# One instruction order for another: weight-block sums moved from batch 0 to batch 1, constants built on chip, one scaling per pair of maxima

## The chip, the cores and the metric

The kernel runs on 1 core of one Trainium2 chip. The metric is the device time of that core in microseconds (us). TensorE is called PE below, VectorE DVE, ScalarE ACT, GpSimd POOL; SP is the queue from which all DMAs are issued, and it issues them strictly in its own order.

## The reference

Windowed attention with block summaries, then a gated feed-forward layer on its output.

```python
B, H, S, D = 4, 8, 768, 64          # block = 32, window = 16
k_sum = k.reshape(B, H, nb, block, D).max(axis=3)      # one key per block of 32
v_sum = v.reshape(B, H, nb, block, D).mean(axis=3)
scores_l = scale * q @ k^T, kept where |i - j| < window, else -1e9
scores_s = scale * q @ k_sum^T + log(block)
a = softmax(concat[scores_l, scores_s]);  attn = a @ concat[v, v_sum]
x = attn as (3072 tokens, 512)
g = x @ w_gate; val = x @ w_val     # 512 -> 1536
out = (g * sigmoid(g) * val) @ w_out                   # 1536 -> 512
```

The three weight matrices arrive as 64-bit floats; everything else is 32-bit.

## The kernel before

**Stages.** The work goes batch by batch (4 batches of 768 tokens, each in two halves of 384, `k = 2 * batch + half`). Per half there are 4 attention units `u`, each two heads. A unit is: `SC` scores on PE, `max0`/`max1` maxima on DVE, a scaling of the maxima by 1/8, six `exp` on ACT, `eps`, `rcp`, `nrm` (normalisation, DVE or POOL), `PP` transposes on PE, `pt` copies out of PSUM, `XO` (weights times values) on PE, and a split of the result into a high and a low part (`xh`, `xl`).

**Feed-forward.** The 1536 inner columns go in 12 chunks `j`. In batch 0 (`u_plain`) a chunk's raw 64-bit weights are loaded (`raw_w`), decoded by ACT and DVE (`abs`, `clamp`, `shift`, `sign`, `low`, each 128x1024) into a tile `m_w`, and split into a high and a low part (`hi` on ACT, `lo` on DVE or POOL, written to the tile `w`). PE then makes three products per pair of parts. In batches 1 to 3 (`u_seven`) a Strassen-like scheme needs 7 block products in place of 8, and for this four sums and differences of 128x256 blocks of each chunk's weights: `weight_sums`, the steps `sumA22`, `sumA21`, `sumA11`, `sumA12`, one after another on the same tile. Before the change they are made in batch 0 on the decoded tile `m_w` (for chunks 0 and 1 on a copy that is loaded again, `m_again`), stored to DRAM (`sf`), and in batch 1 loaded (`ls`, into the tile `s`), split (`sh`, `sl`) and stored again (`ss`) for batches 2 and 3. `down` makes the last product; its banks are called `acc`.

**What sets the order.** Each step is recorded with the engines that may do it and a cost. A planner (`order`, `run`) lays all steps out in time by these costs, after `nudge` has moved single steps by a written table of numbers (`NUDGES`); each engine then executes its steps in exactly that order. Where the planner saw PE idle in the first 110 us, it fills in warm-up matmuls on a tile `warm`.

**Start.** Constants (`raw_parts`: masks and logarithms that PE adds to the scores through `parts_sb` and an identity `id_r`; `id_sb`; `mean_sb`, the block means' matrix) are loaded by DMA. The first units on PE are SC(0,1), SC(0,3), then `pv` (block means of the values, `first_means`).

## Time and profile before

| what | value |
|---|---|
| timed runs | 678.13 us median of 3 (677.75 to 681.1) |
| profiled execution, its own time | 681.53 us |
| its span, first to last instruction | 679.8 us |
| busy share of the span | PE 98%, DVE 76%, ACT 50%, POOL 18% |
| mean granted TensorE clock | 0.995 of full speed |

The profile is of one execution; a busy PE is a stream of matmuls whose ends are modelled, so it shows gaps in the stream and not how fast the stream is. The three timed runs and the profiled one lie 3.8 us apart.

### The profile page before, as it was taken

Reading aid. Unit: us, or ns where it says so; the run is one execution under the profiler, and the core shown is the slowest. Engines: PE = TensorE matmul, PEld = TensorE weight load, DVE = VectorE, ACT = ScalarE, POOL = GpSimd, SP = SyncE. Lnnn points to the kernel's source line nnn. Section 1 sums busy time; section 2 is a strip of 40 time slices with the busy share of each in tenths; the row PEclk is TensorE's granted clock in tenths of the full one; section 3 lists DMA queues with packets and bytes.
Section 4 is the critical chain, followed back from the end, with each engine's and each line's share of the span. In section 5 each row is a group of like instructions: output and inputs, shape, how many; then the busy total and the mean of one; then the engine's idle time right before and its main releaser. Section 6 shows DMA issues by size and latency. Waiting matters only on the chain.

```text
span 679.8 us, 13325 instructions
## 1 busy us (share of the span) xinstructions
PE 667.9 (98%) x5097; PEld 616.2 (91%) x5097; DVE 513.2 (76%) x1135; ACT 340.8 (50%) x850; POOL 124.4 (18%) x115
## 2 busy tenths in 40 slices
PE   8999999999999999999999999999999999999997
PEld 8789899899899998989999898989999898989896
DVE  4899998999999786977758883766768762646464
ACT  2888757677664386644544265744535233313130
POOL 0615306504412130112413140100001000000000
PEclk8999999999999999999999999999999999999999
DMA  9999558878657588785957584663715462535232
GB/s 326 374 341 351 186 215 305 319 273 286 226 200 256 219 283 289 256 282 198 279 227 232 189 301 144 248 212 136 248 39 204 181 221 104 218 108 217 109 109 93
DMA packets 40111, 153.06 MB, mean 225 GB/s; under 512 B 4400, under 2 KB 9328, under 8 KB 33136
## 3 DMA queue, kind: packets, MB, share of 16 engines
q1 hardware_dynamic: 40048, 152.21, 63.5%
q8 instruction: 40, 0.66, 0.4%
q14 instruction: 23, 0.19, 0.1%
HBM read 116.54 MB, written 35.65 MB: 224 GB/s over the span
## 4 chain that ended last, share of the span: by engine, by line
PE 76%; DVE 11%; DMA 7%; issue 2%; ACT 2%; POOL 1%; SPq 0%; DVEq 0%; ACTq 0%; POOLq 0%
PE p L1105 37%; PE acc L1177 25%; PE g L1064 4%; PE v L1064 3%; PE sc L598 3%; PE xo L747 2%; PE pp L714 2%; DVE m_w L949 1%; DVE m_w L943 1%; DMA s<-ss 1%; DMA kw<-in_kW 1%; DMA s<-sf 1%; DVE w L489 1%; DMA raw_w<-in_wgv 1%; DVE m_w L930 1%
## 5 line engine op out<-in xcount | busy, mean ns | idle before, releaser
L1177 PE MATMUL acc<-o,hh 128*128 128x512 f32 x570 | 177.3, 392 | 0.0
L1177 PEld LDWEIGHTS acc<-o,hh 128*128 128x128 f32 x570 | 105.7, 188 | 21.9 <-issue 1.0
L1105 PE MATMUL p<-xh_T,s 128*128 128x384 f32 x432 | 122.6, 339 | 0.9 <-DVE s L489 0.4
L1177 PE MATMUL acc<-o,hl 128*128 128x512 f32 x285 | 111.4, 391 | 0.0
L1105 PE MATMUL p<-xh_B,wa 128*128 128x384 f32 x288 | 84.8, 335 | 0.0
L1105 PEld LDWEIGHTS p<-xh_T,s 128*128 128x128 f32 x432 | 79.0, 188 | 3.1 <-DMA s<-ss 1.1
L484 ACT COPY s<-p 128x384 f32<-128x384 f32 x61 | 29.2, 479 | 90.5 <-PE p L1105 83.3
L1105 PE MATMUL p<-xl_T,s 128*128 128x384 f32 x216 | 72.3, 335 | 0.0
L489 DVE TENSOR_TENSOR part<-acc,part 128x512 f32<-128x512 f32 x71 | 47.5, 685 | 29.0 <-PE acc L1177 29.0
L1177 PEld LDWEIGHTS acc<-o,hl 128*128 128x128 f32 x285 | 53.5, 188 | 11.6 <-DVE hl L489 0.3
L641 ACT ACTIVATE p<-p,nm 128x120 f32<-128x120 f32 x144 | 55.2, 385 | 11.7 <-DVE nm L629 10.2
L489 DVE TENSOR_TENSOR c<-p,u 128x384 f32<-128x384 f32 x72 | 39.6, 552 | 20.2 <-PE p L1105 20.2
L1064 PE MATMUL g<-xh_B,w 128*128 128x384 f32 x192 | 54.1, 340 | 0.4 <-DVE w L489 0.3
L1064 PE MATMUL v<-xh_B,w 128*128 128x384 f32 x192 | 53.2, 335 | 0.0
L1105 PEld LDWEIGHTS p<-xh_B,wa 128*128 128x128 f32 x288 | 53.0, 188 | 0.1
L484 ACT CAST hh<-a 128x384 fp32r<-128x384 f32 x47 | 24.1, 514 | 51.5 <-DVE a L489 47.6
L489 DVE TENSOR_TENSOR hl<-a,hh 128x384 fp32r<-128x384 f32 x77 | 45.9, 596 | 3.6 <-ACT hh L484 0.4
L1105 PE MATMUL p<-xl_B,wa 128*128 128x384 f32 x144 | 48.1, 334 | 0.0
L489 DVE TENSOR_TENSOR a<-c,a 128x384 f32<-128x384 f32 x65 | 40.7, 626 | 5.1 <-ACT a L1040 2.5
L1105 PE MATMUL p<-xh_B,s 128*128 128x384 f32 x144 | 42.4, 334 | 0.0
L1105 PE MATMUL p<-xh_T,wa 128*128 128x384 f32 x144 | 42.3, 334 | 0.0
L1105 PEld LDWEIGHTS p<-xl_T,s 128*128 128x128 f32 x216 | 40.6, 188 | 0.3
(151 smaller groups left out, 1353.8 us busy)
## 6 DMA issues: line engine op xcount, KB each, us to landing
wa<-wa SPq DMA_DIRECT2D x36, 768.0 KB, 4.3
s<-ss SPq DMA_DIRECT2D x24, 1024.0 KB, 7.2
raw_w<-in_wgv SPq DMA_DIRECT2D x12, 1024.0 KB, 6.6
ss<-s SPq DMA_DIRECT2D x12, 1024.0 KB, 7.6
wa<-w SPq DMA_DIRECT2D x12, 768.0 KB, 5.5
kw<-in_kW SPq DMA_DIRECT2D x24, 360.0 KB, 5.6
vw<-in_vW SPq DMA_DIRECT2D x28, 288.0 KB, 4.9
kt<-in_kP SPq DMA_DIRECT2D x16, 400.0 KB, 5.5
```

The costliest lines, as they stand in the source:

```text
L484: nc.scalar.copy(out, in_)
L489: vector[e].tensor_tensor(out=out, in0=a, in1=b, op=op)
L598: nc.tensor.matmul(make(sc[h])[s * QT : (s + 1) * QT, c * KC + at : c * KC + at + x.shape[-1]], make(q)[hs, qs], x, start=not biased or c ...
L641: nc.scalar.activation(out=make(p)[:, i, :], in_=make(p)[:, i, :], func=AF.Exp, scale=-1.0, bias=make(nm)[:, i : i + 1], accum_out=make(sm ...
L714: nc.tensor.transpose(make(pp)[:KC, c * P : (c + 1) * P], make(p)[:, g * NT // 2 + c, :], make(id_sb))
L747: nc.tensor.matmul(ps[hs, qs], v, make(pt)[:, h, qs], start=True, stop=True)
L930: lambda e: nc.vector.tensor_scalar(out=make(m), in0=make(m), scalar1=F64_LO, scalar2=F64_HI, op0=ALU.max, op1=ALU.min), (), (m,),
L943: lambda e: nc.vector.scalar_tensor_tensor(out=bits(), in0=high(), scalar=-0x40000000, in1=bits(), op0=ALU.bitwise_and, op1=ALU.bitwise_or ...
L949: lambda e: nc.vector.scalar_tensor_tensor(out=bits(), in0=low(), scalar=29, in1=bits(), op0=ALU.logical_shift_right, op1=ALU.bitwise_or), ...
L1064: nc.tensor.matmul(t[:, :TOK], a, x, start=u == order_of[0] and i == 0, stop=u == order_of[-1] and i == 2,)
L1105: nc.tensor.matmul(t[:, :TOK], a, x, start=first and kk == 0 and n == 0, stop=kk == 1 and n == 2, skip_group_check=not first,)
L1177: nc.tensor.matmul(ps[:, :wide], a, w, start=j == js[0] and m == 0, stop=j == js[-1] and m == 2)
```

## The change

Six things change. (1) For chunks 3 to 11 the four block sums are no longer made in batch 0. The decoded tile goes to DRAM as it is, and batch 1 loads it into a new tile `sm` (one buffer), makes the sums there, and splits from it. Chunk 2 is as before; chunks 0 and 1 are loaded again for their sums at chunks 10 and 11 and no longer at 5 and 6. (2) In batch 0 the six maxima of a unit are scaled by one instruction after both maxima, and not by one for each three. (3) The three constants are made by memsets and by POOL's `affine_select`, and their DMAs are gone. (4) The planner lets a step on DVE, ACT or POOL that waits for a DMA start 2.5 us later than it thinks the DMA lands (`SAFE`, for landings between 60 and 215 us). (5) Where a step may go to several engines, DVE is charged 0.3 us more than before, and `join` may now go to ACT. (6) The table of nudges is another one.

```diff
+BY_EXP = 0
+ONE_SCALE = True
+SUMS_LATER = 3
-AGAIN = 5
+AGAIN = 10
...
+SAFE, SAFE_FROM, SAFE_TO = 2.5, 60.0, 215.0
-BIAS = {DVE: 0.0, ACT: 0.0, POOL: 0.3}
+BIAS = {DVE: .3, ACT: 0.0, POOL: 0.3}
...
-kt(0,1) -217.9; q(0,1) -205.2; raw_parts -367.5; id_sb -346.1; mean_sb -133.9; vn(1) -330; vr(1) -256.6
+kt(0,1) -92.5; q(0,1) -47; kt(0,3) -57; q(0,3) +18.5; kt(0,0) +51.4; q(0,0) +23.5; kt(0,2) +55.6; vn(0) +57.9
...
+        more = SAFE if s.engine == DMA and SAFE_FROM < s.end < SAFE_TO else 0.0
         for o in s.next:
-            at[o] = max(at[o], (s.end + lag) if o.after[s] else s.start)
+            at[o] = max(at[o], s.end + lag + more * (not {PE, DMA} & set(o.engines)) if o.after[s] else s.start)
...
+    def add_choose(name, b, part, cols, to, pattern, base, keep, other, rows=1):
+        plan.add(
+            name, {POOL: 0.1 + 0.0012 * cols},
+            lambda e: nc.gpsimd.affine_select(
+                out=to(), in_=to(), pattern=pattern, compare_op=keep, fill=other, base=base, channel_multiplier=rows,
+            ), (), ((b, part),),
+        )
+
+    def make_constants():
+        masks = lambda: make(raw_parts)[:, : 3 * KC].rearrange("p (v c) -> p v c", c=KC)
+        add_fill("id one", id_sb, None, P, lambda: make(id_sb), 1.0)
+        add_choose("id here", id_sb, None, P, lambda: make(id_sb), [[-1, P]], 0, ALU.is_equal, 0.0)
+        logs = log_parts()
+        for x, to in enumerate((lambda: masks()[:, :, KW:], lambda: make(raw_parts)[:, 3 * KC : 3 * KC + NB], lambda: make(raw_parts)[:, 3 * KC + NB :])):
+            add_fill(f"log{x}", raw_parts, f"l{x}", NB, to, logs[x])
+        add_fill("mask none", raw_parts, "m", 3 * KW, lambda: masks()[:, :, :KW], 0.0)
+        for s in range(2):
+            rows = slice(s * QT, (s + 1) * QT)
+            to = lambda rows=rows: masks()[rows, :, :KW]
+            add_choose(f"mask{s} above", raw_parts, "m", 3 * KW, to, [[0, 3], [-1, KW]], 2 * WIN - 1, ALU.is_ge, MASK)
+            add_choose(f"mask{s} below", raw_parts, "m", 3 * KW, to, [[0, 3], [1, KW]], -1, ALU.is_ge, MASK, rows=-1)
+        add_fill("mask first", raw_parts, "m", WIN, lambda: masks()[:QT, 0, :WIN], MASK)
+        add_fill("mask last", raw_parts, "m", WIN, lambda: masks()[QT:, 2, WIN + QT : KW], MASK)
+        add_fill("mean all", mean_sb, None, NV * NB, lambda: make(mean_sb), 1.0 / BLK)
+        add_choose("mean above", mean_sb, None, NV * NB, lambda: make(mean_sb), [[P, NV], [-BLK, NB]], -WIN, ALU.is_ge, 0.0)
+        add_choose("mean below", mean_sb, None, NV * NB, lambda: make(mean_sb), [[-P, NV], [BLK, NB]], WIN + BLK - 1, ALU.is_ge, 0.0, rows=-1)
...
-                plan.add(f"scl{g}({k},{u})", {DVE: 0.14, ACT: 0.18}, lambda e, g=g: shrink(e, g), (), ((nm, g),))
+                if not ONE_SCALE:
+                    plan.add(f"scl{g}({k},{u})", {DVE: 0.14, ACT: 0.18}, lambda e, g=g: shrink(e, g), (), ((nm, g),))
+                elif g == 1:
+                    plan.add(f"scl({k},{u})", {DVE: 0.14, ACT: 0.18}, lambda e: shrink(e, None), (), (nm,))
...
-            weight_sums(j, m)
+            if j < SUMS_LATER:
+                weight_sums(j, m)
+            keep_sums(j, m)
...
-            add_dma(f"ls({b},{j})", P * NC * 4, lambda: lo().bitcast(F32), lambda: make(SF[j]), (SF[j],), ((s, 1),))
-            add_copy(f"sh({j})", (ACT, DVE), NC, hi, lambda: lo().bitcast(F32), ((s, 1),), ((s, 0),))
+            whole, part = (lambda: lo().bitcast(F32)), (s, 1)
+            if j >= SUMS_LATER:
+                part = buf("tmp", "sm", [P, NC], f"sm{j}", room="tmp")
+                whole = lambda part=part: make(part)
+            add_dma(f"ls({b},{j})", P * NC * 4, whole, lambda: make(SF[j]), (SF[j],), (part,))
+            if j >= SUMS_LATER:
+                weight_sums(j, part)
+            add_copy(f"sh({j})", (ACT, DVE), NC, hi, whole, (part,), ((s, 0),))
             plan.add(
                 f"sl({j})", on((DVE, POOL), "tt", NC),
-                lambda e: minus(e, lo(), lo().bitcast(F32), hi().bitcast(F32)), ((s, 0),), ((s, 1),),
+                lambda e: minus(e, lo(), whole(), hi().bitcast(F32)), ((s, 0), part) if j >= SUMS_LATER else ((s, 0),), ((s, 1),),
```

The order moves at many places. The first shown is the start of the SP queue. `kt` are a unit's keys, `q` its queries, `vn` value rows, `raw_w` a chunk's raw weights. Before:

```order
L503 DMA raw_parts<-in_parts 128x408
L503 DMA id_sb<-in_ident 128x128
L503 DMA vn_99<-in_vN 128x1536
L503 DMA vn_99<-in_vR 32x256
L503 DMA kt_1_106<-in_kP 128x800
L503 DMA q_1_108<-in_qP 128x384
L503 DMA kt_3_110<-in_kP 128x800
L503 DMA mean_sb<-in_mean 128x168
```

And after the change:

```order
L496 DMA kt_1_107<-in_kP 128x800
L496 DMA kt_3_119<-in_kP 128x800
L496 DMA q_1_127<-in_qP 128x384
L496 DMA vn_131<-in_vN 128x1536
L496 DMA vn_131<-in_vR 32x256
L496 DMA q_3_172<-in_qP 128x384
L496 DMA q_0_174<-in_qP 128x384
L496 DMA q_2_176<-in_qP 128x384
```

The constants' DMAs are gone and unit 1's queries stand third in the queue and no longer sixth, behind two loads of keys.

The second place is DVE's start after the change, with the semaphores that each row waits for. The first rows fill the constants; `ks` are a unit's block keys, without which its scores can't be finished.

```order
L519 MEMSET raw_parts 128x3x24
L519 MEMSET raw_parts 128x3x96
L519 MEMSET raw_parts 128x24
L519 MEMSET mean_sb 128x168
L519 MEMSET raw_parts 64x16 [waits DVE_49,Pool_49]
L519 MEMSET raw_parts 64x16 [waits Pool_49]
L568 TENSOR_REDUCE ks_1_133<-kt_1_107 128x24 [waits DMAHW0_49]
L568 TENSOR_REDUCE ks_3_135<-kt_3_119 128x24 [waits DMAHW1_49]
```

The two 64x16 fills are new, wait for POOL's seven selections, and stand in DVE's queue ahead of the first `ks`.

The third place is DVE in batch 1, around chunk 4: `s_4` is that chunk's split tile, `sm_3328` the tile of chunk 5, `c`, `a`, `u`, `hl` are work on the feed-forward of chunks 2 and 3. Before:

```order
L489 TENSOR_TENSOR s_3_3207<-s_3_3207 128x1024 [waits DVE_49]
L489 TENSOR_TENSOR hl_2_1_3316<-a_2_1_3294,hh_2_1_3307 128x384 [waits Activation_49]
L817 TENSOR_REDUCE vr_2_3320<-vt_2_2534 128x24 [waits DMAHW4_49]
L486 CAST s_4_3271<-s_4_3271 128x1024 [waits DMAHW6_49,DMAHW1_49]
L489 TENSOR_TENSOR s_4_3271<-s_4_3271 128x1024 [waits DVE_49]
```

And after the change:

```order
L482 TENSOR_TENSOR hl_2_1_3302<-a_2_1_3259,hh_2_1_3296 128x384 [waits Activation_49]
L479 COPY part_0_3309<-acc_0_0_3220 128x512 [waits PE_49]
L482 TENSOR_TENSOR s_4_3304<-sm_3193,s_4_3304 128x1024 [waits DMAHW4_49,Activation_49]
L846 TENSOR_REDUCE vr_3_3326<-vt_3_3281 128x24 [waits DMAHW0_49]
L482 TENSOR_TENSOR sm_3328<-sm_3328 128x256 [waits DMAHW2_49,DVE_49]
L482 TENSOR_TENSOR sm_3328<-sm_3328 128x256 [waits DVE_49] x3
L482 TENSOR_TENSOR u_1_3_3396<-p_1_3_3363,s_1_3_3394 128x384 [waits Activation_49]
```

Four sums of chunk 5 now stand on DVE one row behind the split of chunk 4, and the load of `sm` for chunk 5 can be issued only when that split is done, since there is one buffer. Over the program the block sums on DVE go from 26 in batch 0 to 8 there and 25 in batch 1; on POOL from 22 to 4 and 11.

## Rows read from the trace of the kernel before

**Rows 1.** The page's busy times over the span: us, share, instructions.

```profile
PE 667.9 (98%) x5097; PEld 616.2 (91%) x5097; DVE 513.2 (76%) x1135; ACT 340.8 (50%) x850; POOL 124.4 (18%) x115
```

**Rows 2.** Stretches (us from the start): length, then busy us of each engine (instructions), granted clock, DMA share, GB/s. The last two are batch 1 and batches 2 and 3.

```profile
36.10:55.30 19.20, 18.17 (x262) 16.75 (x258) 19.20 (x29) 16.39 (x41) 4.20 (x4) 1.00 0.97 361
55.30:82.00 26.70, 25.71 (x243) 23.07 (x244) 26.21 (x43) 20.71 (x50) 14.48 (x11) 1.00 0.72 247
82.00:119.00 37.00, 37.00 (x244) 35.23 (x243) 32.20 (x68) 23.64 (x49) 10.21 (x8) 1.00 0.74 259
119.00:153.00 34.00, 33.77 (x263) 30.30 (x262) 33.80 (x74) 24.10 (x55) 11.30 (x10) 1.00 0.83 295
153.00:221.00 68.00, 67.50 (x561) 61.76 (x560) 66.71 (x153) 42.33 (x102) 22.61 (x19) 1.00 0.71 242
226.10:382.60 156.50, 156.05 (x1158) 143.93 (x1157) 121.48 (x293) 82.62 (x213) 35.67 (x32) 1.00 0.74 253
382.60:673.40 290.80, 290.33 (x1875) 270.62 (x1874) 183.07 (x430) 110.69 (x271) 12.56 (x15) 1.00 0.48 170
```

**Rows 3.** What PE waited for: us in total, times, longest.

```profile
PE sc L598 <- DMA q<-in_qP: 1.3, 1, 1.3
...
PE g L1064 <- DVE xl_B L489: 0.9, 1, 0.9
```

**Rows 4.** PE in order of time (start, us, what): the first scores of SC(0,1) and of SC(0,3), the two `pv`, the first `g`.

```profile
8.97 0.35 PE L598 MATMUL sc<-kt,q 64*64 64x96 f32 x2 [1.32 <-DMA q<-in_qP]
...
11.38 0.62 PE L598 MATMUL sc<-kt,q 64*64 64x96 f32 x8
...
15.02 3.31 PE L772 MATMUL pv<-vn,mean_sb 128*24 128x128 f32 x28
...
21.68 1.83 PE L772 MATMUL pv<-vn,mean_sb 128*24 128x128 f32 x28
...
36.14 0.44 PE L1064 MATMUL g<-xh_B,w 128*128 128x384 f32 x1
```

**Rows 5.** Stretches of the start, columns as in rows 2; the last number is GB/s.

```profile
0.00:6.00 6.00, 4.96 (x29) 4.97 (x30) 0.67 (x3) 1.28 (x1) 0.19 (x4) 1.00 0.63 190
6.00:7.00 1.00, 1.00 (x11) 1.00 (x11) 0.00 (x0) 0.00 (x0) 0.00 (x0) 1.00 1.05 380
0.00:16.00 16.00, 13.61 (x164) 12.88 (x166) 6.67 (x14) 3.96 (x14) 0.19 (x4) 0.86 0.89 319
11.40:18.20 6.80, 6.80 (x85) 5.52 (x84) 3.84 (x10) 2.16 (x12) 0.00 (x0) 0.50 1.03 410
```

**Rows 6.** DMA issues: count, KB of each, median us from issue to landing.

```profile
raw_w<-in_wgv SPq DMA_DIRECT2D x12, 1024.0 KB, 6.6
...
kt<-in_kP SPq DMA_DIRECT2D x16, 400.0 KB, 5.5
q<-in_qP SPq DMA_DIRECT2D x32, 192.0 KB, 5.7
...
vn<-in_vN SPq DMA_DIRECT2D x2, 768.0 KB, 7.3
```

**Rows 7.** The chain of work that ended last (start, us, what): its first transfer, and the load and split of one chunk's sums in batch 1.

```profile
3.04 5.80 DMA q<-in_qP
...
313.33 7.02 DMA s<-sf
...
321.10 1.24 DVE s L489
322.38 7.57 PE p L1105 x42
```

**Rows 8.** DVE in order of time: the first block keys `ks`, the first `lo` of a weight chunk, and the low part of the last unit of half 1.

```profile
8.34 0.95 DVE L542 TENSOR_REDUCE ks<-kt 128x24 f32<-128x768 f32 x1 [0.54 <-DMA kt<-in_kP]
...
34.73 1.21 DVE L489 TENSOR_TENSOR w<-m_w,w 128x1024 fp32r<-128x1024 f32 x1
...
80.89 0.54 DVE L489 TENSOR_TENSOR xl_B<-xo,xh_B 128x384 fp32r<-128x384 f32 x1
```

**Rows 9.** Instructions on the decoded tile `m_w`: count, ns min/median/max, first and last start, shape. The 128x256 rows are the block sums.

```profile
L489 DVE TENSOR_TENSOR m_w<-m_w x22: 405/411/1224, 60.1 to 205.5; 128x256 f32<-128x256 f32 x22
L489 POOL TENSOR_TENSOR m_w<-m_w x18: 732/1080/3275, 54.2 to 195.9; 128x256 f32<-128x256 f32 x18
L926 ACT ACTIVATE m_w<-raw_w x12: 1122/1156/1212, 23.6 to 192.2; 128x1024 f32<-128x1024 f32 x12
...
L943 DVE SCALAR_TENSOR_TENSOR m_w<-raw_w,m_w x12: 1176/1216/2348, 28.1 to 196.8; 128x1024 int32<-128x1024 int32 x12
...
L484 ACT CAST w<-m_w x12: 1045/1052/1092, 32.4 to 199.6; 128x1024 fp32r<-128x1024 f32 x12
```

**Rows 10.** POOL in order of time: a one-input copy of 384, the first two-input instruction of the run (720 wide), and a later one of the same shape.

```profile
20.75 0.50 POOL L486 COPY vw<-vn 64x384 f32<-64x384 f32 x1
...
26.86 1.70 POOL L693 TENSOR_TENSOR p<-p,ri 128x720 f32<-128x720 f32 x1
...
66.47 1.38 POOL L693 TENSOR_TENSOR p<-p,ri 128x720 f32<-128x720 f32 x1
```

**Rows 11.** Between 222 and 400 us, all DMAs into or out of `s`: issue to landing.

```profile
DMA to landing us min/median/max: 3.9/7.0/11.2
```

**Rows 12.** What DVE waited for between 222 and 400 us: us in total, times, longest.

```profile
DVE s L486 <- DMA s<-sf: 2.9, 3, 1.7
```

159 lines of the change are left out of this document (83 added, 76 removed).

## The prediction

> **What bounds it now.** I read the busy times first: PE is busy 98% of the span, DVE 76% [rows 1]. With PE near full, a change pays only where PE's stream has gaps, so I cut the span into stretches [rows 2]. From 82 us to 673.4 us PE idles 0.50 us up to 153, 0.50 up to 221, 0.45 in batch 1 and 0.47 in batches 2 and 3: about 2 us in 591. Between 36.1 and 82 us it idles 1.03 + 0.99 us. Before 36 lies the long start: the first scores wait for their queries until 8.97 us, and the first feed-forward product `g` begins at 36.14 [rows 4]. The waits say what ends the start's gaps: first the DMA of `q`, at the end of the start the low part `xl_B` from DVE [rows 3]. DVE is busy 19.20 of 19.20 us between 36.1 and 55.3, and 26.21 of 26.70 up to 82 [rows 2], and the `xl_B` that PE waits for ends at 81.43 [rows 8]. So up to 82 us the kernel goes by DVE, which was fed late; behind that, by PE's own work, which the change leaves as it is. PE's matmuls are the same in number and shape in both orders.
>
> The profiled execution took 681.53 us: 679.80 of span and 1.73 around it. That is 3.40 above the median of the timed runs. I make the sum against 681.53 and carry the difference over to 678.13.
>
> **Step 1, the queue's start.** Unit 1's queries stood behind 204 + 64 + 768 + 32 + 400 KB, with their own 192 KB 1660 KB = 1.70 MB (sizes of `kt`, `q` and `vn` [rows 6], the others from their shapes). The queue moved 1.14 MB in 6 us and then 0.38 a us [rows 5], so their bytes were through at 7.5; they landed at 3.04 + 5.80 = 8.84 [rows 7], 1.35 later. After the change 400 + 400 + 192 KB = 1.02 MB stand in front: through at about 5.6, landed at 7.0. SC(0,1) can begin 1.9 us sooner, if its keys and constants are there.
>
> The constants now come from POOL: seven selections of 4 x 288 + 128 + 2 x 168 = 1616 elements a row, an operation that no row shows. The nearest rows bound it: a copy of 384 took 0.50 us (1.3 ns an element), a block sum of 256 1.08 us at the median (4.2 ns) [rows 9, 10]. That gives 2.1 to 6.8 us; a selection has one input, as the copy, so I take 3. POOL then ends at about 4, between 3 and 7.5. Two fills on DVE wait for it, and behind these stands `ks` with 0.95 us [rows 8]: PE has what it needs between 4.1 and 8.6. At 3 us the making is hidden under the `q` transfer; without that cover it costs at most 8.6 - 7.0 = 1.6, and still nothing against 8.97.
>
> **Step 2, the first weights.** With 4 keys, 4 queries and both value tiles ahead, 4992 KB = 5.11 MB go through until the first `raw_w` is there. The queue had moved 319 x 16 = 5.1 MB at 16 us [rows 5], so it lands at 17.4. Chunk 0 is decoded alone, no longer abreast with chunk 1: `abs` 1.16 to 18.6, two scalings and two combinations of 1.2 on DVE among other rows to about 23.5 [rows 9]. ACT has the third `raw_w`'s `abs` ahead of `hi`; that load ends with 7.21 MB, at 0.41 a us [rows 5] at 21.1 + 1.35 = 22.4, so `hi` ends at 22.4 + 1.16 + 1.05 = 24.7 and `lo` at 26. Before, the first `lo` ended at 35.94 [rows 8].
>
> This is not 10 us won: DVE did other chunks' rows meanwhile. The fair mark is the last `xl_B`. In the order, DVE has 70 rows between the first `lo` and it before, and 78 after. Before, they took 81.43 - 35.94 = 45.5 us, 0.65 a row; 78 rows take 50.7, and from 26 that gives 76.7: 4.7 us sooner. The eight further rows hold more normalisations and fewer small rows than the mean; counted by kind they are some 1.5 us dearer, which leaves 3.2. I take 4.0, with 1 (PE or a transfer is late next and holds DVE) and 6.5 (all rows of DVE come at once) as bounds.
>
> **Step 3, the sums leave batch 0.** 26 sums on DVE become 8: 18 x 0.41 = 7.4 us. 22 on POOL become 4: 18 x 1.08 = 19.4 us [rows 9]. Nearly all lies behind 82 us, where PE has 37.00 of 37 us, 33.77 of 34 and 67.50 of 68 [rows 2]. The work that hides it is PE's own stream; the most that can come back is 0.73 us and the small hitches within the stream. I take 1.0, bounds 0 and 2. The reserve behind DMAs and the bias to ACT only say who does what when; DVE is busy 33.80 of 34 and 66.71 of 68 us there [rows 2], so it hardly waits for a DMA, and they too are worth at most this. The scaling removes eight small instructions, and lets three `exp` of a unit wait for the second maximum; DVE is ahead of ACT in both orders: 0.
>
> **Step 4, the sums come to batch 1.** 25 x 0.41 = 10.3 us on DVE, 11 x 1.08 = 11.9 on POOL. DVE has 156.5 - 121.5 = 35 us free there [rows 2], so the load fits. What matters is the loop of the single `sm` buffer: load 7.0 [rows 11], four sums 1.6 (DVE) to 3.0 (two of them on POOL), `sh` 1.05 as a cast of this size on ACT [rows 9], `sl` 1.24 [rows 7]: 10.9 to 12.3 us. PE takes 156.5 / 12 = 13.0 for a chunk. It fits, with 1 to 2 us to spare. Behind the first sum that waits in DVE's queue stands `u` of the next chunk, and PE waits for its bank. Before, DVE waited 2.9 us in three places on this load [rows 12], and the 7.02 us load on the chain let PE start at 322.38 [rows 7]. I charge 0.5, bounds 0 and 4.
>
> **Sum.** 681.53 - 4.0 - 1.0 + 0.5 = 677.0; against the median 678.13 - 4.5 = **673.6 us**.
>
> TensorE's clock was at half (1.2 GHz) from 11.4 to 18.2 us [rows 5], after PE had idled before 8.97; `pv` took 3.31 us there and 1.83 later [rows 4]. After the change the ten warm-ups ahead of SC(0,1) are gone and PE idles longer before it, so such a stretch may come again or fall otherwise. PE's work in it grows by some 2 to 3 us; it is covered as long as DVE sets the end of the start. If not, up to 3 us of step 2 are lost, which its lower bound holds.
>
> **Rivals.**
> *The constants are late* (0.10). What speaks for it: DVE's `ks` stands behind POOL. If POOL needs 6 us more than I take, SC(0,1) starts at 4 + 6 + 1.1 = 11.1, 2.1 later than before; step 2's gain is gone, the first attention is 2 us late, of which the early `raw_w` hides part: about 678 to 680, say 679. Against it: the first two-input instruction on POOL, in front of which a configuration instruction stands in the order of before, took 1.70 us beside 1.38 of a later one [rows 10], so 0.3 for the first call. The Trainium skill (GPSIMD Engine Reference, Instruction dispatch) says that a first call to freshly loaded code costs about 6 us that no instruction shows; by that rule this rival comes true. The trace does not agree with it for that first call.
>
> *The start's gain is given back* (0.10). DVE is ahead, but the next `raw_w` can only come when PE has freed a slot, so DVE waits and is where it was. For it: DVE's load to the last `xl_B` is the same in sum. Against: PE too is ahead by then. 681.53 - 0.5 carries over as 677.6.
>
> *Batch 1 stalls: slower* (0.16). If the load of `sm` takes 10 us, between the median and the longest of 11.2 [rows 11], the loop is 10 + 3.0 + 1.05 + 1.24 = 15.3, 2.3 over PE's 13.0. Nine chunks make 20.7; one chunk's products, 7.57 us [rows 7], are buffered, so 13 us arrive: 673.1 + 13 = 686. It begins to cost at a loop of 13.9 and makes the kernel slower by 0.5% at 14.8, a load of 9.5. For it: one buffer, DMAs in order in one queue. Against: half of the transfers on `s` landed in 7.0 us or less, and the tile's load no longer waits for a slot of `s`.
>
> *More is won* (0.12): the full 6.5 of step 2 and 2 of step 3, and 0 for step 4: 678.13 - 8.5 = 669.6.
>
> **How the numbers follow.** My forecast has 0.52 and spans 671 to 676.6 by the nearer half of its bounds. A measurement of this kernel tells about 0.5% (3.4 us) from no change, so faster is below 674.7. Of the 0.52, 0.38 lie there and 0.14 in no change. Faster: 0.38 + 0.12 = 0.50. Same: 0.14 + 0.10 + 0.10 = 0.34. Slower: 0.16. The range leaves out a part of the slower case and the far end of the better one: 667.5 to 681.
>
> **What would show it.** Step 1: SC(0,1) at about 7, POOL's selections over by 5, `q` landing at 7. Step 2: the first `lo` ends at 26, `g` begins at 31 to 34, and the last `xl_B` ends near 77. Step 3: PE's busy time between 82 and 221 no fuller than now. Step 4: DVE waits for `sm` of 1 to 3 us and PE waits below 1. I'd be wrong if PE's gaps in batch 1 sum to several us, if selections begin only at 7 us, or if DVE idles before 80 us.

## The result and the profile after

| kernel | median (spread, runs) | before beside it | ratio, 95% interval |
|---|---|---|---|
| changed | 684.12 us (682.63 to 684.75, 6) | 678.26 us (median of 6) | 1.0075 [1.0059, 1.009] |

The change makes the kernel slower by 5.9 us; 673.6 was predicted, with a range up to 681. The profiled execution took 684.49 us, 682.7 of them span. Of all executions below, one of a_xo took 1590.25 us, at full clock; its ratio leaves that one out, and no run says why.

The page's busy times after, to be held against [rows 1]:

```profile
PE 667.3 (98%) x5077; PEld 614.0 (90%) x5077; DVE 503.9 (74%) x1087; ACT 378.5 (55%) x905; POOL 127.4 (19%) x129
```

DVE lost 9.3 us of work and ACT gained 37.7, as the change says. PE's share says nothing; the stretches do. After, columns as in [rows 2]:

```profile
55.30:82.00 26.70, 24.84 (x300) 21.56 (x299) 26.21 (x42) 20.61 (x49) 6.24 (x5) 1.00 0.70 242
82.00:119.00 37.00, 37.00 (x246) 35.50 (x245) 36.33 (x71) 25.85 (x51) 2.34 (x3) 1.00 0.79 282
119.00:153.00 34.00, 34.00 (x268) 31.03 (x267) 33.87 (x66) 23.24 (x51) 12.66 (x9) 1.00 0.75 260
153.00:221.00 68.00, 67.33 (x562) 61.93 (x561) 56.80 (x135) 41.66 (x103) 16.88 (x16) 1.00 0.74 255
226.10:382.60 156.50, 154.01 (x1142) 140.96 (x1142) 125.30 (x294) 98.55 (x236) 51.90 (x51) 1.00 0.73 247
```

Batch 0 is a little fuller (0.23 us more between 119 and 153), its end not, and in batch 1 PE idles 2.49 us instead of 0.45. What PE waited for, columns as in [rows 3]:

```profile
PE pp L743 <- DVE p L722: 2.5, 3, 1.3
PE sc L624 <- DMA q<-in_qP: 2.1, 1, 2.1
...
PE p L1161 <- DVE v L482: 1.1, 1, 1.1
...
PE acc L1233 <- DVE hl L482: 0.7, 1, 0.7
...
PE p L1161 <- DVE part L482: 0.4, 1, 0.4
```

The first two are the start (PE waits for the normalisation `nrm`, the tile `p`, at 31.88, 34.98 and 53.14 us); the other three are new and lie in batch 1. PE in order of time, answering [rows 4]; a bracket is the idle time ahead of a row and what ended it:

```profile
8.03 0.42 PE L624 MATMUL sc<-kt,q 64*64 64x96 f32 x8 [2.12 <-DMA q<-in_qP]
...
10.84 2.91 PE L1274 MATMUL sc<-warm 128*128 128x128 f32 x12
13.68 0.62 PE L624 MATMUL sc<-kt,q 64*64 64x96 f32 x8
...
213.70 1.62 PE L776 MATMUL xo<-pt,vw 120*64 120x64 f32 x48
...
226.54 0.42 PE L1161 MATMUL p<-xh_T,s 128*128 128x384 f32 x1 [0.42 <-DVE part L482]
...
242.04 0.45 PE L1161 MATMUL p<-xh_B,s 128*128 128x384 f32 x1 [1.10 <-DVE v L482]
...
376.47 0.50 PE L1233 MATMUL acc<-o,hl 128*128 128x512 f32 x1 [0.69 <-DVE hl L482]
```

SC(0,1) starts at 8.03 and not at 7; SC(0,3) at 13.68, later than the 11.38 of before, because a warm-up group stands ahead of it. DVE in order of time, answering [rows 8]: the first `lo`, the last `xl_B` of the start, and the rows that PE waited for.

```profile
29.32 1.23 DVE L482 TENSOR_TENSOR w<-m_w,w 128x1024 fp32r<-128x1024 f32 x1
...
81.39 0.55 DVE L482 TENSOR_TENSOR xl_B<-xo,xh_B 128x384 fp32r<-128x384 f32 x1
...
214.66 0.56 DVE L479 COPY xf<-xo 128x384 f32<-128x384 f32 x1 [1.85 <-PE xo L776]
...
225.72 1.27 DVE L482 TENSOR_TENSOR part<-acc,part 128x512 f32<-128x512 f32 x2
...
240.82 0.69 DVE L479 CAST s<-s 128x1024 fp32r<-128x1024 f32 x1 [2.89 <-DMA q<-in_qP]
...
375.05 1.36 DVE L482 TENSOR_TENSOR hl<-a,hh 128x384 fp32r<-128x384 f32 x1
```

The first `lo` ends 5.4 us sooner than before (30.55 against 35.94), and the last `xl_B` 0.5 us later.

**Where the time went.** The matmuls are the same in every order, so I give each shape its usual length in the stream (128x384: 173 ns), add them up without the warm-ups (649.7 us in all), and ask when each trace has done a given amount. This is an estimate: with other lengths for the small shapes the differences between traces move by up to half a microsecond or so. The columns are the time at 60 us of work (the start is over), what 60 to 200 takes (batch 0), 200 to 340 (batch 1) and 340 to 400 (its end and the beginning of batch 2).

| trace | to 60 | 60-200 | 200-340 | 340-400 | span |
|---|---|---|---|---|---|
| before | 84.0 | 141.3 | 140.2 | 60.0 | 679.8 |
| before again | 84.0 | 140.3 | 139.5 | 60.0 | 678.3 |
| after | 84.6 | 139.6 | 142.2 | 62.1 | 682.7 |
| after again | 84.8 | 139.6 | 141.0 | 62.2 | 683.7 |

From the table: the start gained nothing, batch 0 some 0.7 to 1.7 us, and the two stretches from 200 to 400 lost 3.0 to 4.8 (3.7 between the two "again" rows). The two "again" rows come from the runs b_again and a_again below; from 400 on, `after` lost nothing against `before`, and a_again some 1.6 us, 1.3 of it in two waits for loads of `s`.

### The profile page after: what moved, and what is told of

It reads as the page before. It is cut to its first block, busy times and chain, and to the rows that moved or that the text cites. A ratio compares the mean times of both kernels' runs of the same rounds, so it can differ in the third digit from the quotient of the medians.

```text
span 682.7 us, 13319 instructions
## 1 busy us (share of the span) xinstructions
PE 667.3 (98%) x5077; PEld 614.0 (90%) x5077; DVE 503.9 (74%) x1087; ACT 378.5 (55%) x905; POOL 127.4 (19%) x129
## 4 chain that ended last, share of the span: by engine, by line
PE 75%; DVE 8%; DMA 3%; ACT 2%; issue 1%; POOL 0%; SPq 0%; DVEq 0%; ACTq 0%
PE p L1161 34%; PE acc L1233 24%; PE g L1119 5%; PE v L1119 4%; PE xo L776 3%; PE pp L743 2%; PE sc L624 2%; DMA s<-sf 1%; DMA s<-ss 1%; DVE xl_T L482 1%; DVE part L482 1%; DVE hl L482 1%; DMA q<-in_qP 1%; DVE xf L482 1%; DVE p L722 0%
## 5 line engine op out<-in xcount | busy, mean ns | idle before, releaser
L477 ACT CAST hh<-a 128x384 fp32r<-128x384 f32 x71 | 36.2, 513 | 63.0 <-DVE a L482 60.2
L482 DVE TENSOR_TENSOR hl<-a,hh 128x384 fp32r<-128x384 f32 x79 | 47.6, 602 | 13.0 <-ACT hh L477 10.5
L482 DVE TENSOR_TENSOR u<-p,s 128x384 f32<-128x384 f32 x36 | 19.9, 554 | 30.0 <-ACT s L477 28.4
L482 POOL TENSOR_TENSOR hl<-a,hh 128x384 fp32r<-128x384 f32 x17 | 20.5, 1211 | 110.6 <-ACT hh L477 63.8
```

Of the source, the lines that this page charges most:

```text
L477: nc.scalar.copy(out, in_)
L482: vector[e].tensor_tensor(out=out, in0=a, in1=b, op=op)
```

## The experiments

Orders are changed behind the planner, by taking named steps out of the finished order and putting them ahead of others (`move(name, ahead_of)`), so that all other steps stay as they were.

### The two kernels again, and the clock of an execution

**b_again** and **a_again** are the kernels unchanged.

> The kernel before once more, unchanged, for a second trace and for the spread of its times. Every theory expects 678.3 us, within 1 us. The first trace of before took 681.5, 3.3 above the median of its runs. If that was a single disturbed execution, this trace has a span near 676.5, and PE in the kernel after the change falls behind it by 5 to 6 us and not by 3; the stretch in which the two traces of before part shows where the 3 us were lost.

> The kernel after the change once more, unchanged: a second trace of it and the spread of its times beside the three below. Every theory expects 684.1 within 1 us. The two earlier traces with its order (without warm-ups, without the sums) lose the same four places: 0.6 us at P7 of chunk 0 (225 us), 0.4 at P7 of chunk 8 (323), 1.1 to 1.3 at the last products of batch 1 (375 to 380); the 1.3 us at 240.6 was in the first trace of after alone. If they are the order's, they stand in this trace too; the one at 240.6 need not.

b_again: 678.7 us, ratio 0.9993 [0.9977, 1.0008]. a_again: 682.59 us (680.21 to 685.43, 8), ratio 1.0052 [1.0032, 1.0073]. So the loss is between 3.4 and 5.9 us.

Each timed execution shows its mean granted clock. In five sets of runs, the 111 executions of before part in two: 85 with 0.998 or more, with medians of 678.3 to 679.0 in a set, and 26 below, with medians of 680.6 to 681.0, so 1.6 to 2.7 us longer, 2.5 in the middle set. Both profiles of before belong to the second kind; their stretch at half clock is [rows 5]. So the prediction's starting point was a start that before has in one execution of four. Two runs show what decides it.

**a_nowarm**, the changed kernel without the warm-ups from SC(0,1) on (the eleven ahead of everything stay):

```diff
-            spare[0] = min(30, max(0, int((s.idle - 0.5) / 0.25)))
+            spare[0] = 0
```

> The kernel after the change, same order, without the warm-up matmuls that are filled in from SC(0,1) on (the eleven ahead of everything stay). Theory 1 (the start's gain is eaten by warm-ups at half clock: the six ahead of SC(0,3) take 2.9 us, 10.8 to 13.7): SC(0,3) begins near 11, the first `lo` 1 to 2 us sooner, and 1 to 3 us of the end are won: 681 to 683. Rival (the start is set by what DVE and ACT get from the queue, and PE only waits where it now warms up): 684.1 within 0.7. A third way, against both: with less work PE stays at half clock longer, and the time grows by 1 to 3 us.

683.81 us (681.05 to 685.5, 8), ratio 1.0061 [1.0038, 1.0084]; all eight executions at 0.995 or less. Its trace is of the fastest, at 0.995; six of the eight ran at 0.984 to 0.989. **b_fill**, before with 15 warm-ups ahead of SC(0,1) and not 10:

```diff
+            if s.name == "SC(0,1)":
+                spare[0] = 15
```

> The kernel before, same order, with fifteen warm-ups ahead of SC(0,1) and not ten, so that PE is busy until its queries land. What it tells: in the kernel before, 12 of 49 timed executions had a mean clock below 0.998 and were 1.6 to 2.6 us slower. If the idle 1.3 us ahead of SC(0,1) brings the half clock on, it is gone here: all clocks at 0.998 or more, median 678.2 to 678.6 and a narrow spread. Its trace is then that of the start of before at full clock: theory 1 (the new start is no faster at equal clock) expects PE's work of the first 84 us to be done 2.0 to 2.6 us sooner than in the slow trace of before, at 81.5 to 82, where the start after the change stood at 82.5 with full clock. Rival (the new start is faster at equal clock): 83 to 84.

678.57 us, ratio 0.9984 [0.9964, 1.0004]; all twelve executions at 0.999 or more. Stretches of the trace of b_fill, then of a_nowarm, then of the changed kernel:

```profile
11.40:18.20 6.80, 5.97 (x142) 5.29 (x141) 5.44 (x15) 4.58 (x25) 2.15 (x3) 1.00 1.03 409
```

```profile
20.00:27.00 7.00, 5.50 (x68) 5.11 (x70) 6.75 (x11) 6.08 (x20) 4.88 (x5) 0.55 1.00 407
```

```profile
9.00:15.00 6.00, 6.00 (x67) 5.72 (x64) 2.19 (x4) 2.37 (x13) 1.45 (x3) 0.50 1.03 404
```

The number before the DMA share is the granted clock: 1.00 where the warm-ups fill PE's wait, 0.55 in a later stretch where there are none, and 0.50 (1.2 GHz) in the changed kernel, behind the 2.12 us that PE waits for `q`. Before and b_fill together show the cause: with PE's wait filled, the slowed executions are gone. The price, some 2.5 us, is the distance between the two kinds of before. It doesn't explain the change: three executions of after at full clock have a median of 683.33, three at less 684.21; for a_again they are 682.3 and 682.88.

### The start

**a_fill**: the changed kernel with 8 warm-ups ahead of SC(0,1) and none, for six, ahead of SC(0,3).

```diff
+            if s.name == "SC(0,1)":
+                spare[0] = 8
+            elif s.name == "SC(0,3)":
+                spare[0] = 0
```

> The kernel after the change with eight warm-ups ahead of SC(0,1), where PE stood idle 2.1 us for its queries, and none ahead of SC(0,3), where six stood. Theory 1 (PE's idle 2.1 us brings the half clock, and that eats the start's gain): the granted clock stays full in most executions, SC(0,3) begins at 10.5 and not at 13.7, and the median falls by 1 to 2.5 us, to 681.6 to 683.1, with a narrower spread. Rival (DVE and ACT set the end of the start, and PE has time to lose): 684.1 within 0.7, with or without the half clock.

682.04 us, ratio 1.0039 [1.0025, 1.0053]: 0.55 us less than a_again beside it, within the intervals. The start's warm-ups are not where the loss is.

**b_onchip**: the old order with the constants made on chip and the first keys and queries drawn forward, and nothing else of the change.

```diff
...
+    for name, do in (("raw_parts", make_parts), ("id_sb", make_id), ("mean_sb", make_mean)):
+        by[name].do = do
+    move("mean_sb", "vn(1)")
+    move("kt(0,1)", "vn(1)")
+    move("q(0,1)", "vn(1)")
```

> The kernel before in its own order, but the three constants are made on chip (same fills and selections as after the change, at the head of DVE's and POOL's rows), their three DMAs are gone, and unit 1's keys and queries go first in the queue. It takes the first step alone. SC(0,1) begins at 7.7 (its ten warm-ups end at 7.6) and not at 8.97; the half clock may fall elsewhere. If the start's lead reaches the end, 677.0 to 677.3; if it is given back, 678.3 within 0.7; if an earlier SC(0,1) only brings the half clock on sooner and longer, 679 to 680.

679.1 us, ratio 1.0016 [0.9993, 1.0038]: the constants on chip neither cost nor win anything that can be measured. Four of its ten executions ran at 0.995 or less (median 681.38), the other six took 678.27.

Stretches from 0 to 36.1 us, of b_again, of after, of b_fill, of a_nosums (below) and of b_on2 (below); DVE's busy time is the fourth number behind the bounds:

```profile
0.00:36.10 36.10, 32.12 (x473) 28.62 (x473) 24.44 (x46) 20.25 (x72) 11.58 (x17) 0.91 0.93 349
```

```profile
0.00:36.10 36.10, 30.54 (x425) 27.67 (x426) 23.97 (x48) 22.12 (x73) 12.44 (x24) 0.91 0.91 334
```

```profile
0.00:36.10 36.10, 32.42 (x492) 29.92 (x493) 26.04 (x48) 21.12 (x73) 10.49 (x17) 1.00 0.95 362
```

```profile
0.00:36.10 36.10, 30.71 (x469) 26.90 (x470) 26.90 (x52) 24.88 (x77) 12.98 (x24) 0.95 0.96 353
```

```profile
0.00:36.10 36.10, 33.00 (x517) 30.35 (x518) 27.59 (x56) 22.99 (x77) 14.27 (x24) 1.00 0.95 364
```

DVE has worked 24.44, 23.97, 26.04, 26.90 and 27.59 us by then, and these traces have done 60 us of PE's work at 84.0, 84.6, 82.3, 81.8 and 81.1: in these five a microsecond of DVE's work done early goes with about one won at the end of the start. It is not exact: b_onchip, with 27.65 us of DVE, stands at 81.8. This is the row that the prediction should have forecast. With a start that is not slowed from 9 us on, the new order (a_nosums 81.8, a_nowarm 82.6, a_fill 82.5) is about level with the old one (b_fill 82.3, b_onchip 81.8). Two things weaken this: the three traces of the new order have a shorter stretch at half clock later, between 16 and 28 us, and those of a_nosums, a_nowarm, b_onchip and b_on2 are each the fastest execution of their run. So an early first `lo` wins little here; that other rows, which come later, pay for it is argued and not shown.

### The sums

**a_nosums** leaves out the 36 block sums of chunks 3 to 11; loads, splits and stores stay.

```diff
+    for j in range(SUMS_LATER, NJ):
+        for x in ("A22", "A21", "A11", "A12"):
+            done.remove(by[f"sum{x} w{j}"])
```

> The kernel after the change, same order, without the 36 block sums of chunks 3 to 11: they are left out of the computation (the scheme of batches 1 to 3 then works on wrong blocks), all loads, splits and stores stay. Theory 2 (step 4 was sized too small: the sums' work on DVE and POOL in batch 1 is what makes PE wait there): the stalls at 240.6 and 375 to 379 us shrink and 3 to 4 us come back: 680 to 681. Rival (what stalls is the order of rows and the landing of loads, which the sums don't touch; the largest stall, at 240.6, is on chunk 2, whose sums were made in batch 0): 683 to 684.1.

682.58 us, ratio 1.0052 [1.0033, 1.0072], between the two ranges expected and nearer the rival's. Without the work that step 4 charges, the kernel is as slow as a_again. PE in order of time in a_nosums shows the same two waits, 2.8 and 4.3 us sooner since its start and some of its stream were shorter:

```profile
223.77 0.41 PE L1161 MATMUL p<-xh_T,s 128*128 128x384 f32 x1 [0.45 <-DVE part L482]
```

```profile
372.18 0.50 PE L1233 MATMUL acc<-o,hl 128*128 128x512 f32 x1 [0.70 <-DVE hl L482]
```

**a_sums0** does the opposite: the changed kernel's order, but each chunk's sums made in batch 0, behind its `lo`.

```diff
...
+            s.do = lambda e, j=j, to=to, x=x, y=y, op=op: tt(e, *(make(MW[j])[:, cols[c]] for c in (to, x, y)), op)
+            move(s.name, f"wa{j}")
+        move(f"sf{j}", f"wa{j}")
```

> The kernel after the change with the 36 block sums of chunks 3 to 11 put back into batch 0, on the engines that had them in batch 1, each behind the chunk's `lo` and ahead of the store; the rest of the order stays. It undoes the first of the six changes alone. My steps 3 and 4 said that batch 0 would pay 1.0 for them and batch 1 be relieved by 0.5. From the run without the sums, where batch 1 gained 0.3 to 0.7, I expect batch 1 to gain 0.5, and batch 0 to lose 0 (if PE's stream hides them, as before the change) or 1 to 3 (if DVE, with fewer free places in this order, makes PE wait): 682.1 to 685.

702.73 us, ratio 1.0331 [1.0296, 1.0367], far outside the range expected. From 82 to 153 us PE is busy 62.77 us of 71 and the longest wait is 6.5:

```profile
82.00:153.00 71.00, 62.77 (x439) 56.63 (x439) 65.11 (x114) 40.75 (x72) 13.31 (x11) 0.93 0.58 201
```

```profile
PE acc L1233 <- DVE part L482: 6.5, 1, 6.5
```

That shows that this order was laid out without room for the sums in batch 0. It doesn't show what they cost an order made for them: before has them there and is busy 70.77 us in the same stretch [rows 2].

### The two ends of batch 1

Two views name what stands ahead of the wait at 226. The engines between 205 and 230 us, in b_again and in a_again (DVE is the fourth number behind the bounds):

```profile
205.00:215.00 10.00, 10.00 (x56) 9.60 (x55) 9.90 (x24) 4.14 (x10) 0.00 (x0) 1.00 0.91 298
215.00:230.00 15.00, 15.00 (x74) 13.25 (x73) 11.13 (x17) 3.68 (x8) 6.77 (x4) 1.00 0.50 192
```

```profile
205.00:215.00 10.00, 10.00 (x89) 9.18 (x89) 4.73 (x11) 3.72 (x9) 0.00 (x0) 1.00 0.53 195
215.00:230.00 15.00, 14.58 (x86) 12.45 (x81) 14.19 (x21) 6.94 (x14) 8.06 (x6) 1.00 0.57 208
```

The old order has DVE busy 9.90 and then 11.13 us; the new one leaves it idle for half of the first ten and fills the next fifteen to 14.19. Part of the reason is one pair of steps. `XO(3,2)` and `XO(3,3)`, the last attention products of batch 0, stood ahead of the last chunk's `g`; the new table puts them behind two of the last six `D0` (the final products of batch 0). b_again's PE:

```profile
202.75 1.62 PE L747 MATMUL xo<-pt,vw 120*64 120x64 f32 x48
```

After, it is 213.70 (above), and the copy `xf<-xo` waits until 214.66. Several of batch 1's first inputs (`t`, `xh_T`, `xl_T`) wait for these copies, so their rows fall together with the `part` rows that empty PE's banks.

**a_mend** moves 16 rows on DVE, ACT and POOL at the three waits, and leaves XO where it is. Four of them:

```diff
...
+        ("T2l(1,0)", "part(0,3,4)"), ("T2l(1,1)", "T4(1,1)"), ("T4(1,0)", "T4(1,1)"), ("T4h(1,0)", "T4(1,1)"),
...
```

> The kernel after the change with 16 rows moved at the three places where PE waits in every trace of its order: the sums into `part` of batch 0 ahead of two low parts of the next batch's blocks, two sums of chunk 7 ahead of a normalisation and of an `hl`, and `hl` of chunk 11 ahead of the next batch's block sums, which go behind it. Nothing else moves. Theory 3 (batch 1 is slower because of where DVE's rows stand, not because the sums are more work): 0.6 + 0.4 + 1.1 come back, 682.0 beside 684.1 of after on this chip. Theory 2 (DVE and POOL have too much to do in batch 1): the rows that are put back are late next, PE waits for them, and less than 0.7 comes back.

682.35 us, ratio 1.0055 [1.0035, 1.0076]: nothing won. PE in order of time, and a stretch:

```profile
375.78 0.39 PE L1233 MATMUL acc<-o,hl 128*128 128x512 f32 x1
378.08 1.20 PE L1233 MATMUL acc<-o,hh 128*128 128x512 f32 x2 [1.92 <-DVE part L482]
379.07 0.63 PE L1233 MATMUL acc<-o,hl 128*128 128x512 f32 x1
...
378.00:380.00 2.00, 1.92 (x5) 1.55 (x6) 2.00 (x5) 0.00 (x0) 0.00 (x0) 0.54 0.57 207
```

The wait moved to the next row of a full DVE and grew, and behind it the same matmul took 0.63 us in place of 0.39 for some 3 us: the granted clock was 0.54 between 378 and 380 us and 0.61 between 380 and 382. So a_mend may have won something at its three places and lost it to this stop; its trace is of one execution.

**a_xo** moves the transposes for both XO back ahead of the last `g`, both XO (in its trace at 208.73) and their copies ahead of the last `v`, the first rows of batch 1 ahead of the last `mul` of batch 0, and rows at the end of batch 1 ahead of others there, 34 steps in all:

```diff
...
+        ("PP0(3,2)", "g(11,1)"), ("PP1(3,2)", "g(11,1)"), ("PP0(3,3)", "g(11,1)"), ("PP1(3,3)", "g(11,1)"),
...
+        ("XO(3,2)", "v(11,1)"), ("XO(3,3)", "v(11,1)"),
...
+        ("T4h(2,1)", "mul(1,11,1)"), ("B22l(2,0)", "mul(1,11,1)"), ("B22l(2,1)", "mul(1,11,1)"), ("T4l(2,1)", "mul(1,11,1)"),
...
```

> The kernel after the change with rows moved at the two batch boundaries. From batch 0 to 1: the transposes and results of the last attention pair, XO(3,2) and XO(3,3), go back ahead of the last `g` and `v` on PE, about where they stood before the change, and seven rows on their results go ahead of the last `mul`. From 1 to 2: `hl` of chunk 11 ahead of the next batch's low parts, as in the run before, but now the three sums into `part` also go ahead of them. Theory 3 (the order leaves DVE idle for 5 us ahead of the boundary and full behind it): the 0.6 us at P7 of chunk 0 and the 1.1 to 1.3 at the last products of batch 1 are gone and nothing takes their place: 680.7 to 681 beside 682.6 of after. Theory 2 (DVE is full there whatever the order): they turn up at another row again, 682.6 within 0.7.

680.63 us, ratio 1.0014 [0.9994, 1.0034], where a_again had 1.0052 [1.0032, 1.0073]; the intervals just touch. Its stretches, and a wait that is left:

```profile
205.00:215.00 10.00, 10.00 (x99) 9.18 (x97) 5.45 (x12) 6.06 (x14) 3.04 (x3) 1.00 0.43 168
215.00:230.00 15.00, 15.00 (x75) 13.32 (x74) 11.61 (x21) 5.00 (x10) 2.96 (x3) 1.00 0.61 226
...
374.00:381.00 7.00, 6.94 (x31) 5.23 (x30) 5.83 (x12) 1.54 (x3) 1.29 (x2) 1.00 0.39 149
...
321.57 0.44 PE L1161 MATMUL p<-xh_T,s 128*128 128x384 f32 x1 [0.22 <-DVE c L482]
```

Behind 215 us DVE has 11.61 us where it had 14.19, PE is full, and the wait near 376 is gone too. In the ten microseconds before, DVE is still idle for almost half: what helped is the relief behind them, not the filling of that idle time. PE's work from 200 to 400, by the table's reckoning:

| before-type: before / b_again / b_on2 | after / a_again / a_nowarm / a_nosums / a_fill / a_mend | a_xo / a_xofill |
|---|---|---|
| 200.2 / 199.5 / 199.5 | 204.3 / 203.2 / 202.8 / 202.9 / 203.6 / 205.6 | 201.2 / 201.2 |

Every trace of the new order takes at least 202.8 there, with the sums or without them; with both ends mended 201.2. So by this reckoning 2.0 us of a_again's 3.7 are the two ends; how they share it was not run. Part of the other 1.7 lies at the wait for `c` of the view above, which stands in after (at 323.92), a_again and a_xo alike and in neither trace of before; no run removes it alone, and the rest stays without a name.

**a_xofill** is a_xo with the warm-ups of a_fill:

> The kernel after the change with both repairs that helped: the rows at the two batch boundaries moved, and eight warm-ups ahead of SC(0,1) in place of six ahead of SC(0,3). If the two causes (the half clock at the start, 0.5 us in the median by the run that filled it, and the order at the boundaries, 2.0 to 2.5) add up and are most of what was lost, it comes to 679.6 to 680.3 beside 678.8 of before, and what is left is below 0.2%. If the clock was the smaller part of the two only because the boundaries hid it, up to 1 us lower; if the repairs don't add, 680.6.

680.08 us, ratio 1.002 [1.0004, 1.0035]: the changed kernel mended at three places is still not faster than before.

### The table against the five other parts

**a_empty** and **b_empty** are the two kernels with an empty table, so that the planner's own order runs:

```diff
-NUDGES = """
...
+NUDGES = """"""
```

> The kernel after the change with an empty table of nudges: the planner's own order with the five other changes in it. Beside the next run it tells whether the changes themselves or the written table lost the time. Theory 3 (it is the table's order that leaves the boundaries badly placed): with neither table the new version is not slower than the old one, by 0 to 4 us faster. Rival (sums in batch 1, the reserve or the bias are bad in themselves): it is 3 us or more slower than the old one without its table. Both are expected above the tuned ones, at 685 to 705.

> The kernel before with an empty table of nudges, to stand beside the run above. Theory 3 expects it at or above the new version without a table, the rival 3 us or more below; both expect 685 to 705.

| | its own table | empty table |
|---|---|---|
| before | 678.45 | 701.44, ratio 1.0336 [1.0316, 1.0355] |
| after | 684.12 and 682.59 | 682.0, ratio 1.0054 [1.0039, 1.007] |

Both were expected at 685 or more, and after with an empty table is below that. Its trace has XO early again:

```profile
201.61 1.62 PE L722 MATMUL xo<-pt,vw 120*64 120x64 f32 x48
```

PE is full from 205 to 230 us, so it is the new table that moved XO. But between 200 and 440 us PE now waits for `v` (0.5 us) and twice for `s` (0.5 and 0.4), and the kernel is no faster: without the table other waits take the place of its two.

**a_esums** is a_empty with the sums back in batch 0 (and chunks 0 and 1 loaded again at 5 and 6), **a_ebias** a_empty without the reserve and the bias:

```diff
-SUMS_LATER = 3
+SUMS_LATER = 12
-AGAIN = 10
+AGAIN = 5
```

```diff
-SAFE, SAFE_FROM, SAFE_TO = 2.5, 60.0, 215.0
+SAFE, SAFE_FROM, SAFE_TO = 0.0, 60.0, 215.0
-BIAS = {DVE: .3, ACT: 0.0, POOL: 0.3}
+BIAS = {DVE: 0.0, ACT: 0.0, POOL: 0.3}
```

> The kernel after the change with an empty table, and one more thing undone: the block sums are all made in batch 0 again (and chunks 0 and 1 loaded again at 5 and 6), as before the change. Without tables the new version took 682.0 and the old one 701.4. Theory 4 (the sums are what fills DVE in batch 0 where no table has fitted them in; my step 3 then had the right mechanism and its price was already paid by the old table): this kernel loses most of the 19.4 us again, 695 to 702. Rival (the bias, the reserve or the start make the difference): 682 to 686.

> The kernel after the change with an empty table and without the reserve behind DMAs (2.5 us made 0) and without the bias of 0.3 us against DVE; the sums stay in batch 1. Theory 4 (the sums make the difference): 682 to 685. Rival (the planner's reserve and bias do): 690 to 702.

691.22 us, ratio 1.0193 [1.0168, 1.0218], and 688.15, ratio 1.0139 [1.0114, 1.0164]: neither fell into a range expected, since both parts count. In the planner's own order the sums in batch 1 are worth 9.2 us, reserve and bias 6.2, all five parts 19.4. But the old table is worth 23.0 us to the old kernel, and the new table nothing to the new one. I read this so: the tuned old order has by its table what the five parts bring to an untuned one, and nothing is left for them to win. No run puts the five parts under the old table, so this is argued from four medians.

### A version that beats both

**b_best** drew all of the start of b_onchip further forward (it also has the three lines shown for b_on2 below), with no warm-ups ahead of SC(0,1) and five behind:

```diff
+    move("kt(0,3)", "vn(1)")
+    move("q(0,3)", "vn(1)")
...
+            if s.name == "SC(0,1)":
+                spare[0] = 0
+            elif s.name == "FV(0)":
+                spare[0] = 5
```

> The kernel before in its own order with constants made on chip, and with the start drawn forward: keys and queries of units 1 and 3 go first in the queue, ahead of the values; the two copies of unit 3's windows that waited for the values stand behind the first softmax; no warm-ups ahead of SC(0,1), five ahead of the second block means. SC(0,1) begins at 5.9 to 6.2, 3 us sooner than before, and SC(0,3) at 8. If an earlier start reaches the end, 676 to 677 beside 678.5 of before; if what is won is given back by the first weights, which come only 1.7 us sooner, 677 to 678.5; if PE's thinner work brings the half clock more often, 679 to 680.

679.26 us, ratio 1.0 [0.9987, 1.0014]. SC(0,1) began at 6.1, but all twelve executions ran at 0.997 or less: PE idled 2.38 us ahead of 16.61, and the clock was 0.66 between 16 and 21. **b_on2** is b_onchip with the ten warm-ups kept, two copies of unit 3 behind the first softmax and two small copies on ACT:

```diff
+    move("odd1(3)", "exp0(0,3)")
+    move("odd2(3)", "max0(0,3)")
+    by["parts"].engine = by["idr"].engine = ACT
```

> The kernel before in its own order, with constants made on chip, unit 1's keys and queries first in the queue, and the two copies that stood in front of its block keys moved behind the first softmax; the ten warm-ups stay and now reach to the scores, so that PE has no idle time before them. It joins the two things that helped the old order: full clock (678.57 where the queue was as before) and 0.5 us of start (82.3 to 81.8 at 84 us of PE's work). Expected 677.7 to 678.2 beside 678.8 of before, all clocks at 0.998 or more. Rival: 678.5, if the start's 0.5 us doesn't reach the end.

677.78 us, ratio 0.9992 [0.998, 1.0004], with 11 of 12 executions at 0.999 or more. One wait of [rows 3] was left, PE in order of time:

```profile
78.61 0.45 PE L1064 MATMUL g<-xl_B,w 128*128 128x384 f32 x1 [1.00 <-DVE xl_B L489]
```

On DVE a 1.21 us row of `m_o` and a 0.94 us `vr` stood ahead of this `xl_B`. **b_final** moves them behind it:

```diff
+    for name in ("low o4", "vpool(1,1)", "hi o4"):
+        move(name, "lo o4")
```

> The kernel before with constants on chip and the start drawn together, as in the run that took 677.8, and with three rows put behind the last low part `xl_B` of half 1, for which PE waited 1.0 us at 78.6 us in that run's trace: `low` of an output weight, a sum over value rows, and `hi` of that weight. `xl_B` can then start at 76.2, when its high part is done, and not at 78.0. If nothing behind the moved rows is waited for, 1.0 us comes off: 676.6 to 677.0 beside 678.5 of before, 0.2 to 0.3% faster. Rival: `low` and `hi` are late next for the first output products, and it stays at 677.8.

677.27 us (676.18 to 679.45, 12), ratio 0.9975 [0.9962, 0.9988]. PE does not wait between 60 and 90 us any more. It is faster than before by a quarter of a per cent, or 1.1 us against before's executions at full clock beside it (678.37), and thus faster than the changed kernel too. It has a full clock at the start, constants on chip, a queue and two copies drawn together and three rows of DVE moved; what each is worth is below what these runs can tell apart.

## Why the prediction was wrong, step by step

**Step 1** was right on the constants and off on the transfer. POOL's first and last selections:

```profile
1.52 0.44 POOL L525 TENSOR_SCALAR_AFFINE_SELECT raw_parts<-raw_parts 64x288 f32<-64x288 f32 x1 [0.47 <-DVE raw_parts L519]
...
3.93 0.44 POOL L525 TENSOR_SCALAR_AFFINE_SELECT raw_parts<-raw_parts 64x288 f32<-64x288 f32 x1
```

They are over at 4.37 (forecast: about 4), and the seven take 2.78 us (forecast: 3). The rival "the constants are late" falls. The extra of about 6 us that the Trainium skill (GPSIMD Engine Reference, Instruction dispatch) states for a first call to freshly loaded code does not show here: POOL idles 0.47 us ahead of the first selection, for a fill on DVE, and it takes 0.44 us like the last. Whether its code was freshly loaded, no trace shows. `q` was to land at 7.0 and landed at 7.90; in the same order it landed at 6.16 in a_nowarm and at 5.63 in a_nosums, so one execution can't settle such a term to better than 2 us.

**Step 2 is the step that failed**: 4.0 us were to come back, and none did. Its own length was right: from the first `lo` to the last `xl_B` 51.4 us pass (30.55 to 81.94; forecast 50.7). But `lo` came at 30.55 and not at 26, 3.5 us later than in a_nowarm (27.09). Its `raw_w` landed at 19.83 and not at 17.4 (18.07 in a_nowarm, 17.40 in a_nosums, with the same queue), but that isn't what held it: in a_xo, which has the same start, `raw_w` landed at 17.93, and still `abs` began at 21.09 and `lo` ended at 30.39. ACT's `abs` stands behind the `exp` rows of SC(0,3), the first of them this, in after:

```profile
17.55 0.36 ACT L691 ACTIVATE p<-sc,nm 128x120 f32<-128x120 f32 x1 [3.23 <-DVE ri L719]
```

In a_fill, whose SC(0,3) is neither at half clock nor behind warm-ups, that row starts at 13.62 and `abs` at 18.22, right behind its load (18.19). More than that, the mark was wrong twice. The 81.43 of before came from a start at half clock; at full clock b_fill's last `xl_B` ends at 79.67, as early as the new order's (79.1 to 79.9 in a_nosums, a_nowarm and a_fill, with their shorter stretches at half clock). And an early row says nothing while DVE's sum does: 23.97 us of work by 36.1 against 24.44. The prediction named the half clock and covered it by "as long as DVE sets the end of the start"; DVE did set it, but DVE's rows waited for PE's, and so the half clock reached them too.

**Step 3** gained 0.7 us to 1.7 against traces that had small stops of their own, and nothing against b_fill and b_onchip (139.6 us for the stretch in them and in after): inside its bounds of 0 to 2.

**Step 4** was right on the sums and wrong on batch 1 as a whole: it charged 0.5 us, and PE idles 2.49 us there where it had waits below 1. The loss lies beside the sums. The loop of `sm` was to take 10.9 to 12.3 us. The loads of `sm` in batch 1 landed after

```profile
DMA to landing us min/median/max: 3.2/3.8/6.4
```

and not 7.0, and POOL's sums took

```profile
L482 POOL TENSOR_TENSOR sm<-sm x10: 729/741/747, 254.8 to 352.3; 128x256 f32<-128x256 f32 x10
```

so it ran with room to spare, and without the sums the kernel is as slow. DVE's waits for `sm`, answering [rows 12], were above the forecast of 1 to 3 us, and cost nothing that a_nosums won back:

```profile
DVE sm L482 <- DMA sm<-sf: 4.5, 2, 4.2
```

The rival "batch 1 stalls: slower" came near with 686 us, but by luck: its loop never ran late. One load did hold PE up: the chain has it, a chunk whose sums were made in batch 0, answering [rows 7]:

```profile
233.11 7.62 DMA s<-sf
```

Its cast on DVE could come only at 240.82 (the row above names a transfer of `q` that ended with it), `v` stands behind it, and PE lost 1.1 us. The second trace of the same kernel has no such stop.

**The sentence behind the loss** is in the first part: behind 82 us the kernel goes "by PE's own work, which the change leaves as it is". I priced new work and new waits of the parts and took the sixth part, the table, for free. It put two products 11 us later and left DVE overfull behind them; that seam and the next took 2.0 of the 3.7 us between 200 and 400, and most of the other 1.7 are not explained. The order was there to be read, and a look at the last steps of batch 0 on PE would have shown it.

**The sizes.** In the profile's terms 677.0 was forecast and 684.49 measured, 7.5 us off. By the table of before and after, step 2 lost 0.6 where it was to win 4.0 (4.6 of the 7.5), the stretches from 200 to 400 lost 4.1 where 0.5 was charged (3.6), and step 3 won 1.7 for 1.0. The other 3 us between 673.6 and 684.12 are the slowed start of before's profile: the sum was made against it and carried over to a median that doesn't have it. One reading was wrong and changed nothing: up to 153 us PE idles 0.23 us in [rows 2] and not 0.50.

## What to carry to other kernels

Where a change swaps a whole order, look at each seam between stages for steps that moved across others, before pricing the parts that have a name; a saving in work off the path is worth nothing, and a few steps that come late at two seams cost some two microseconds here. Forecast the sum of the bounding engine's work by a fixed time, not the time of one early row. And check first whether the profile shows the ordinary execution: here the mark came from a start that three runs in four don't have.
